# Hedgehog linear attention with a causal convolution gate on one core: value columns copied on GpSimd, batch 3's loads freed, the last output block in halves, and a new order of all work

## The chip, the cores and the metric

The kernel runs on one core of a Trainium2 chip. A core has five engines that run side by side, each through its own instruction queue in order: TensorE (PE, matmuls, with weight loads PEld shown apart), VectorE (DVE), ScalarE (ACT), GpSimd (POOL) and SyncE (SP, here a queue that issues DMAs). The metric is the device time of one execution in microseconds (us); the median of several runs counts.

## What is computed

There are 8 batches, 8 heads, 576 positions and head width 64; a feature map has 128 columns. Cut to what matters, the reference is:

```python
def phi(x):
    proj = einsum('bhsd,df->bhsf', x, w_phi)
    proj = proj - max(abs(proj), axis=-1, keepdims=True)
    return concatenate([exp(proj), exp(-proj)], axis=-1)
q_p, k_p = phi(q), phi(k)
kv  = einsum('bhsf,bhsd->bhfd', k_p, v);  z = sum(k_p, axis=2)
x   = einsum('bhsf,bhfd->bhsd', q_p, kv) / (einsum('bhsf,bhf->bhs', q_p, z)[..., None] + 1e-06)
x   = x.transpose(0, 2, 1, 3).reshape(B, S, 512)
gate = sigmoid(causal 5-tap convolution of x along s, one set of taps per column)
out  = (gate * (x @ w_val)) @ w_out
```

## The kernel before, in words

Each batch passes through the same chain of tasks. A batch's 4608 rows of q and of k lie as 18 chunks of 128 columns by 2 rows; `UNITS` groups the chunks into five units (four of 4 chunks and one of 2), so most tasks exist once per unit `u`. The names below are the ones the texts use, `name(b, u)` with batch and unit.

- q, k and v come by DMA (`load`, L550, on POOL for batches 1 to 7; `loadv`, L531, for v; `load32`, L525 and L527, on SP for batch 0). q and k must be transposed: in batch 0 and 1 by PE (`tp32`, `tp16`) with a copy out of PSUM (`tc32` L542 and L544, `tc16` L560), from batch 2 on by a transposing DMA (`xpose`, L565, on SP).
- `kp` and `qm` (L577, PE) project k and q with w_phi. `kmax` and `qmax` (L585, DVE) take the maxima of the absolute values. `kexp` (L595, ACT) takes exp of plus and minus the projection, so twice per unit. `ek` (L604, ACT) turns the maxima of k into factors, and `vs` (L610 and L611, POOL) scales v by them, four times per batch (head group, sign).
- `st` (L620, PE) sums k features times scaled v over positions; `kv` (L628 on DVE or L632 on ACT) brings the sums out of PSUM.
- The maxima of q are transposed by PE (`mqt`), negated by DVE (`mqr`, L667 in batch 0, L670 later) and spread by POOL (`rx`, L682; batch 0 may do one on DVE, L685). `qp` (PE) projects q again (L693) and adds the spread maxima (L698). `qexp` (ACT, L706; L709 for the last unit) takes the exps.
- `num` (L719, L726, PE) multiplies q features with the sums; `nrm` (L737, L740, DVE) divides. `xtp` (L748, L752, PE, or `xtd`, a DMA, L755) transposes x, `xtc` (L628 or L632) copies it out, `halo` (L768, L769, POOL) sets the convolution's edge columns.
- `gate` (L781, PE) is the convolution, 20 matmuls per column block `j`; `tanh` (L785, ACT) replaces the sigmoid; `val` (L791, PE) is x times w_val; `gv` (L797, DVE) multiplies the two; `gvc` (L805, POOL) gathers the last 32 rows of a batch.
- `out` (L813, PE) multiplies by w_out, four blocks of 128 positions per batch, and every second batch a fifth block (L817) for the remainders of two batches; `oev` (L630 on DVE or L634 on ACT) brings a block out of PSUM, halved; `odma` (L830, L836) stores it.

The weights for `val` are kept in `WV`, 512 columns and then the first 64 columns once more, because `val` reads 128 columns from a start that moves by 64. `c_wv` (L459, a DMA on POOL) loads the 512; `c_wvx` (L462) copies the extra 64. `c_wo` (L465) loads w_out, `c_dupo` (L469 to L471, three DMAs on SP) makes a shifted copy of it. `c_gt` (L486, POOL) builds the convolution's taps in two halves.

The order is not left to a scheduler at run time. `build` makes a list of some 1060 tasks with engines, planned durations and dependences; a planner that is not in the file has put them in a row, and the row is written out: `ORDER` lists the task numbers, `FLEX` gives a letter for every task that two engines could do (A for ACT, D for DVE, P for POOL), `BANKS` the PSUM banks, and `WARM` filler matmuls with no use but to keep PE busy, as "place:bank:size" ("z" fillers add zeros to a bank in use). The instructions are emitted in that row, so each engine's queue follows it. The dependences and durations in `build` only informed the planner: on the chip an instruction waits for the data and buffers that it truly uses, and for what stands ahead of it in its own queue. Where the text says "POOL does a, b, c", it is this row, filtered for POOL.

POOL before, around the loads of batch 3: `c_gt(1)`, `rx(1,4)`, `rx(1,3)`, `rx(1,0)`, `c_gt(0)`, `rx(1,1)`, `c_wv`, `rx(1,2)`, `holdx(2)` (a one-column copy, L512, that waits for batch 2's transposed q), `c_wo`, `vs(1,0,0)`, `vs(1,0,1)`, `load('q',3)`, `load('k',3)`, `vs(1,1,0)`, `halo(0)`, `vs(1,1,1)`, then the `rx` of batch 2. SP before: `xpose` of k and q of batch 2, `loadv(2)`, `c_wvx`, `c_dupo`, `xpose` of k and q of batch 3.

Of the kernel before, what the change touches and what calls it, by code (L numbers as in the profile page):

```python
# [18 lines left out]
DM = 512  # L19
P = 128  # L20
# [15 lines left out]
    "16:3:1 16:3:1 16:3:0 16:3:0 16:3:0 16:3:0 16:3:0 16:3:0 16:3:0 16:3:0 16:3:0 16:3:0 16:3:0 16:3:0 16:3:0 16:3:0 16:3:0 "  # L36
    "16:3:0 50:2:2 71:7:9 73:z80:1 76:0:1 82:z93:1 85:4:2 88:4:3 125:0:1 175:z232:1 181:6:1 191:4:2 206:0:1 216:2:1 "
# [42 lines left out]
)  # L80
FLEX = (
    "DADADAAAAADDPPPPDDDDAADDDDDDDDDDDDDAAADAAAADDDDAAADDDAADAAADDADAADDDDADDDDADDDDDDAADADDAAAAAA"
)
BANKS = (
    "672372616101454523232323016723676705012367230101455672345323010123454501452330176470701456745010145450145676723014501454"
    "501677014576601230167676745677773467232367232345456701676723232367674545014452353623670101232345454452230145450167676767"
    "010123014501230167450120167365012345236745454555723014545234567232323010123236745230167232346701432010167454567010120656"
    "701456701012301670123010167232367674567123677260123230123230167475644501016701670123676745672345232345450123670156672345"
    "010167452345742345670145670101674545012345012367452345010137452301670101452360167"
)  # L90


# [70 lines left out]
def build(plan, em=None):  # L163
# [16 lines left out]
    for b in range(B):  # L180
# [165 lines left out]
        for c in range(5):  # L346
            if c == 4 and b % 2 == 0:
                continue
# [550 lines left out]
```

## Time and profile before

| What | Value |
|---|---|
| Median of 3 runs | 214.34 us (213.82 to 215.61) |
| The profiled execution, its own time | 215.87 us |
| Its span, first to last instruction | 214.1 us |
| PE busy, share of the span | 193.5 us, 90% |
| ACT busy | 178.9 us, 84% |
| DVE busy | 170.3 us, 80% |
| POOL busy | 133.1 us, 62% |
| Bytes moved | 39.90 MB, mean 186 GB/s |
| Last matmul ends | about 208.5 us |

Rows of the profile are read like this. A timeline row gives the start, the duration, the engine and line, the operation, what it writes and reads, how many instructions were merged, and in brackets the idle time before them and what ended it; "issue" there means that the engine waited for nothing that the profile shows. A row of a group gives, behind the bar, busy time, mean ns of one, and the idle time before them. A row of DMA issues ends with the KB of one and the median us from issue to landing. A row of stages gives start and end, length, busy time and count for PE, PEld, DVE, ACT and POOL, then granted clock (1.00 is full), DMA share and GB/s.

### The profile page before, as it was taken

What the parts mean: (1) busy time and instruction counts of PE and PEld (TensorE: products, weight loads), DVE (VectorE), ACT (ScalarE), POOL (GpSimd) and SP (SyncE); (2) the same over time, 40 slices, a digit from 0 to 9 for tenths busy, and PEclk for the clock granted to TensorE, in tenths of its full rate; (3) what the DMA queues carried; (4) which work ended last, traced back from release to release, by engine and by line L of the source; (5) the groups of instructions that cost most, each with busy time, mean ns of one, the idle gap of its engine ahead of it and who ended that gap; (6) DMA issues with size and microseconds to landing.
All of it is one profiled execution on the core that took longest, in us unless ns stands there. A gap on an engine that the chain in (4) does not pass through costs nothing.

```text
span 214.1 us, 8769 instructions
## 1 busy us (share of the span) xinstructions
PE 193.5 (90%) x3809; PEld 137.1 (64%) x3829; DVE 170.3 (80%) x258; ACT 178.9 (84%) x265; POOL 133.1 (62%) x173
## 2 busy tenths in 40 slices
PE   7888687887999999989999999999999999999990
PEld 6554476565665866677667767567667756787630
DVE  3799979994899979988999779998699897653510
ACT  2899989996999899998899997998898988535250
POOL 3645999992957477954995199805991979110100
PEclk9999979999999999999999999999999999999999
DMA  6999989999699699999997979989961363872176
GB/s 194 355 265 210 305 147 202 240 200 193 131 181 271 103 154 269 281 190 162 214 287 133 150 137 275 160 181 207 254 207 45 88 196 73 124 163 65 52 208 184
DMA packets 49953, 39.90 MB, mean 186 GB/s; under 512 B 34165, under 2 KB 39541, under 8 KB 49914
## 3 DMA queue, kind: packets, MB, share of 16 engines
q1 hardware_dynamic: 43616, 28.65, 58.1%
q0 software_dynamic: 6032, 10.49, 26.0%
q8 instruction: 30, 0.49, 0.9%
q10 hardware_dynamic: 266, 0.21, 0.3%
q14 instruction: 9, 0.07, 0.1%
HBM read 30.48 MB, written 9.44 MB: 186 GB/s over the span
## 4 chain that ended last, share of the span: by engine, by line
PE 52%; ACT 19%; DVE 8%; DMA 8%; issue 6%; POOL 5%; SPq 0%; ACTq 0%; DVEq 0%; POOLq 0%
PE PS L791 12%; PE PS L813 10%; PE PS L781 9%; ACT QTIL L706 9%; ACT KTIL L595 7%; PE PS L719 6%; DMA VN<-in_v_dram 6%; PE PS L620 4%; POOL VT L610 3%; PE PS L577 3%; DVE MK L585 3%; PE PS L693 2%; PE PS L817 2%; DMA W<-in_w_phi_dram 2%; PE PS L698 2%
## 5 line engine op out<-in xcount | busy, mean ns | idle before, releaser
L595 ACT ACTIVATE KTIL<-PS 128x1024 bf16<-128x1024 f32 (+1 forms) x80 | 72.2, 968 | 3.9 <-PE PS L577 2.0
L610 POOL TENSOR_TENSOR VT<-VN,EK 128x1152 bf16<-128x1152 f32 x32 | 67.9, 2121 | 4.7 <-DMA VN<-in_v_dram 3.3
L706 ACT ACTIVATE QTIL<-PS 128x1024 bf16<-128x1024 f32 x64 | 62.9, 1056 | 1.4 <-PE PS L698 1.3
L682 POOL TENSOR_TENSOR RX<-MQR,ident 128x512 bf16<-128x512 bf16 (+1 forms) x39 | 36.6, 962 | 36.3 <-DVE MQR L670 34.2
L585 DVE TENSOR_REDUCE MK<-PS 128x8 f32<-128x1024 f32 (+1 forms) x40 | 43.9, 1111 | 2.4 <-ACT KTIL L595 1.4
L585 DVE TENSOR_REDUCE MQP<-PS 128x8 bf16<-128x1024 f32 (+1 forms) x40 | 43.4, 1109 | 1.2 <-PE PS L577 0.7
L791 PE MATMUL PS<-XT,WV 128*128 128x288 bf16 x256 | 34.8, 286 | 0.3 <-DVE KV L628 0.2
L797 DVE SCALAR_TENSOR_TENSOR GV<-TH,PS 128x576 bf16<-128x576 bf16 x32 | 23.8, 752 | 10.2 <-PE PS L791 4.6
L813 PE MATMUL PS<-WOUT,GV 128*128 128x512 bf16 x110 | 29.5, 380 | 1.1 <-issue 0.2
L791 PEld LDWEIGHTS <-WV 128*128 128x128 bf16 x256 | 23.8, 98 | 7.8 <-issue 1.3
L785 ACT ACTIVATE TH<-PS 128x576 bf16<-128x576 f32 x32 | 20.4, 664 | 9.1 <-PE PS L781 6.1
L620 PE MATMUL PS<-VT,KTIL 64*128 64x65 bf16 x1152 | 23.9, 194 | 1.6 <-POOL VT L611 0.6
L620 PEld LDWEIGHTS <-KTIL 64*128 64x128 bf16 x1152 | 21.7, 97 | 4.1 <-issue 2.6
L781 PE MATMUL PS<-XT,GW 64*64 64x288 bf16 x640 | 22.8, 285 | 0.8 <-DVE RCP L737 0.5
L740 DVE TENSOR_TENSOR XN<-PS,RCP 128x512 bf16<-128x512 f32 x32 | 22.1, 691 | 1.2
L719 PEld LDWEIGHTS <-QTIL 128*128 128x128 bf16 x512 | 18.2, 97 | 7.1 <-issue 4.9
L719 PE MATMUL PS<-KV,QTIL 128*128 128x65 bf16 x512 | 20.3, 194 | 0.8 <-ACT QTIL L706 0.5
L781 PEld LDWEIGHTS <-GW 64*64 64x64 bf16 x640 | 17.8, 106 | 3.0 <-issue 1.2
L634 ACT ACTIVATE OUTS<-PS 128x512 f32<-128x512 f32 x22 | 13.5, 620 | 7.3 <-PE PS L813 6.1
L813 PEld LDWEIGHTS <-GV 128*128 128x128 bf16 x128 | 11.2, 98 | 11.4 <-issue 0.6
L577 PE MATMUL PS<-W,qT 64*128 64x128 bf16 x288 | 15.3, 217 | 1.9 <-ACT KTIL L595 0.4
L577 PE MATMUL PS<-W,kT 64*128 64x128 bf16 x288 | 15.1, 223 | 1.9 <-DVE MQP L585 1.1
(79 smaller groups left out, 224.4 us busy)
## 6 DMA issues: line engine op xcount, KB each, us to landing
out_dram<-OUTS SPq DMA_DIRECT2D x32, 256.0 KB, 3.5
VN<-in_v_dram SPq DMA_DIRECT2D x7, 1152.0 KB, 6.6
KQN<-in_q_dram POOLq DMA_DIRECT2D x6, 576.0 KB, 8.4
KQN<-in_k_dram POOLq DMA_DIRECT2D x6, 576.0 KB, 10.0
KTIL<-in_k_dram SPq DMA_DIRECT2D x4, 288.0 KB, 4.1
VN<-in_v_dram POOLq DMA_DIRECT2D x1, 1152.0 KB, 19.3
KTIL<-in_q_dram SPq DMA_DIRECT2D x4, 256.0 KB, 5.1
out_dram<-OUTS SPq DMA_DIRECT2D x14, 64.0 KB, 2.8
```

The costliest lines, as they stand in the source:

```text
L577: nc.tensor.matmul(self.PS[:, t.grp.banks[par], i * P:(i + 1) * P], X[rows, (c0 + i) * P:(c0 + i + 1) * P], self.W2[rows, :], start=True, ...
L585: self.nc.vector.tensor_reduce(o, self.two(t.grp, n * P).rearrange("p a (c f) -> p a c f", f=F), AX.X, ALU.max, apply_absolute_value=True)
L595: self.nc.scalar.activation(self.KTIL[b % 2][:, s, c0:c0 + n, :, :].rearrange("p c a f -> p a c f"), self.two(t.grp, n * P).rearrange("p a ...
L610: nc.gpsimd.tensor_tensor(self.VT[g][:, s, :, 0:D], self.VN[b % 2][:, NC * g:NC * g + NC, :], e.to_broadcast([P, NC, D]), ALU.mult)
L620: nc.tensor.matmul(self.PS[:, t.grp.banks[ab], (s * 2 + x) * E1:(s * 2 + x + 1) * E1], self.KTIL[b % 2][rows, s, J // 2, J % 2, :], self.V ...
L682: self.nc.gpsimd.tensor_tensor(o, *wide(self.MQR[self.mq(b, u)][:, :], self.ident2), ALU.mult)
L706: self.nc.scalar.activation(o, i, AF.Exp, scale=1.0 - 2.0 * s)
L719: nc.tensor.matmul(self.PS[:, t.grp.banks[h // 4], (h % 4) * E1:(h % 4 + 1) * E1], Q[:, s, c % 2, h, (c // 2) * P:(c // 2 + 1) * P], self. ...
L781: self.nc.tensor.matmul(self.PS[o * D:(o + 1) * D, t.grp.banks[par], 0:R], self.GW[r, jj, 4 - m, :], X[r, 4 * a + jj, :, HALO - 8 * s:HALO ...
L791: self.nc.tensor.matmul(self.PS[:, t.grp.banks[par], 0:R], self.WV[:, i, (2 * j + par) * D:(2 * j + par + 2) * D], X[:, 4 * par + i, :, HA ...
L797: nc.vector.scalar_tensor_tensor(out=self.GV[b % 3][:, j, :, :], in0=self.TH[j][:, :, :], scalar=1.0, in1=self.two(t.grp, R), op0=ALU.add, ...
L813: nc.tensor.matmul(self.PS[:, t.grp.banks[0], :], GV[:, j, c % 2, (c // 2) * XH:(c // 2) * XH + P], self.WOUT[:, j, c % 2, :], start=(j == ...
```

## The change

Four things change in the code, and then the whole row of tasks.

1. `c_wvx` is a copy by GpSimd instead of a DMA on SP.
2. In the planner's dependences, batch 3's q and k loads no longer follow `c_wo`; both follow `holdx(2)`.
3. Batch 7's block 3 of the output is computed, brought out and stored in two halves of 256 columns (`outh`, `oevh`, `odmah`), each stored by SP or ACT as its letter says.
4. `FLEX` may now hold S for SP.
5. `ORDER`, `FLEX`, `BANKS` and `WARM` are new. The fillers go from 41 matmuls (18 places at the start, then 12) to 20 (17 at the start, then 3).

```diff
 WARM = (
-    "16:3:1 16:3:1 16:3:0 [16:3:0 fifteen times more] 50:2:2 71:7:9 73:z80:1 76:0:1 82:z93:1 85:4:2 88:4:3 125:0:1 175:z232:1 181:6:1 191:4:2 206:0:1 216:2:1 "
+    "16:6:1 16:6:1 16:6:0 [16:6:0 fourteen times more] 47:7:1 84:0:1 174:2:2 "
 )
...
-                    hx = A("lk", b, 1, "POOL", 0.85, fn("c_wo"), [hx], lat=0.6)
-                    cx = A("lk", b, 1, "DMA", 3.4, None, [hx])
+                    cx = A("lk", b, 1, "POOL", 0.85, fn("c_wo"), [hx], lat=0.6)
+                    cx = A("lk", b, 1, "DMA", 3.4, None, [cx])
...
-                    first = [hx] + first
...
-                cx = A("wvx", 0, 0, "SP", 0.56, fn("c_wvx"), [cx], rank=-440)
-                cx = A("wvx", 0, 0, "DMA", 2.0, None, [cx], rank=-440)
+                cx = A("wvx", 0, 0, "POOL", 0.4, fn("c_wvx"), [cx], rank=-440)
...
     def c_wvx(self, t):
-        self.nc.sync.dma_start(self.WV[:, :, DM:DM + D], self.WV[:, :, 0:D])
+        self.nc.gpsimd.tensor_copy(self.WV[:, :, DM:DM + D], self.WV[:, :, 0:D])
...
+    def outh(self, t, b, c, z):
+        GV = self.GV[b % 3]
+        for j in range(4):
+            self.nc.tensor.matmul(self.PS[:, t.grp.banks[0], 0:DM // 2], GV[:, j, c % 2, (c // 2) * XH:(c // 2) * XH + P],
+                                  self.WOUT[:, j, c % 2, z * DM // 2:(z + 1) * DM // 2], start=(j == 0), stop=(j == 3))
+    def oevh(self, t, b, c, z):
+        o = self.OUTS[out_seq(b, c) % NO][:, z * DM // 2:(z + 1) * DM // 2]
+        self.ev(t, o, self.PS[:, t.grp.banks[0], 0:DM // 2], 0.5)
+    def odmah(self, t, b, c, z):
+        eng = self.nc.scalar if t.eng == "ACT" else self.nc.sync
+        r = slice(z * DM // 2, (z + 1) * DM // 2)
+        d = self.out_d[b].rearrange("(k x y a) o -> a k y x o", k=2, x=8, a=2)[c % 2, c // 2, 0:16, :, r]
+        eng.dma_start(d, self.OUTS[out_seq(b, c) % NO][:, r])
```

The new row, put into words where the prediction speaks of it:

- DVE at the start: the copies of k's units 0 and 1, `kmax(0,0)`, `kmax(0,1)`, `qmax(0,0)`, `qmax(0,1)`, `kmax(0,2)`, `qmax(0,4)`, the first `mqr`, `qmax(0,3)`, `qmax(0,2)`, the copy of k's unit 4, the second `mqr`. Before: the copies of k's units 0 and 2, `kmax` 0 and 1, `qmax` 1 and 0, the copy of unit 4, the first `mqr`, `kmax` 3 and 2, `qmax` 3, 2 and 4, `kmax(0,4)`, the second `mqr`.
- POOL at the start: four `rx` of batch 0 and then its four `vs`; the fifth `rx` (unit 3) is on DVE. Before: two `rx`, one `vs`, two `rx`, three `vs`; the `rx` on DVE was that of unit 4.
- POOL around batch 3's loads: `rx(1,0)`, `rx(1,1)`, `c_gt(1)`, `c_wv`, `rx(1,4)`, `rx(1,2)`, `rx(1,3)`, `holdx(2)`, `vs(1,0,1)`, `load('q',3)`, `c_wo`, `vs(1,0,0)`, `load('k',3)`, `c_gt(0)`, `c_wvx`, `halo(0)`, `vs(1,1,1)`, `vs(1,1,0)`, then the `rx` of batch 2. SP: `xpose` of k and q of batch 2, `loadv(2)`, `c_dupo`, `xpose` of k and q of batch 3.
- From DVE to ACT, up to the last `qexp` of batch 7: output evictions on ACT 17 instead of 13, wide XT copies 3 instead of 2, narrow ones 3 instead of 2, `kv` 5 instead of 4, and the narrow copy of batch 1's q.
- End of PE: `out(7,2)`, the remainder block `out(7,4)`, then the two halves of block 3, second half first. Both halves are brought out by DVE; ACT stores the second half after its two stores of `out(7,4)`, SP the first half after its two.

More of the change, by code (lines that the diff above doesn't have):

```diff
@@ L35 @@
 WARM = (
-    "16:3:1 16:3:1 16:3:0 16:3:0 16:3:0 16:3:0 16:3:0 16:3:0 16:3:0 16:3:0 16:3:0 16:3:0 16:3:0 16:3:0 16:3:0 16:3:0 16:3:0 "
-    "16:3:0 50:2:2 71:7:9 73:z80:1 76:0:1 82:z93:1 85:4:2 88:4:3 125:0:1 175:z232:1 181:6:1 191:4:2 206:0:1 216:2:1 "
+    "16:6:1 16:6:1 16:6:0 16:6:0 16:6:0 16:6:0 16:6:0 16:6:0 16:6:0 16:6:0 16:6:0 16:6:0 16:6:0 16:6:0 16:6:0 16:6:0 16:6:0 "
+    "47:7:1 84:0:1 174:2:2 "
 )
@@ L43 @@
 ORDER = (
[36 rows of a table removed]
[36 rows of a table added]
 )
 FLEX = (
-    "DADADAAAAADDPPPPDDDDAADDDDDDDDDDDDDAAADAAAADDDDAAADDDAADAAADDADAADDDDADDDDADDDDDDAADADDAAAAAA"
+    "DDAADAAAAADDPPPDPDADADDADDDDDADADDDAAAAAADDADADAAADDDAAADAADDDDDAADAAAADADDDDDDDAAAAADDAAADDSDAA"
 )
 BANKS = (
[L85 to L89, printed above, removed]
+    "454616507701234523232323672345672305670167236767452670101123010123456701452370425445201456701010145670101016767456745454"
+    "501016456745267014501676745677773567232367452345676723012301232367674545015452343623670101232345454432230145450167672367"
+    "016767014501230167014530167264012345236745454555023014545234567232323010123236745230167230146701435010167234567010131666"
+    "701456701012301670123010167232367674567723676300123230123230167425544501016701670123676745234545232345450123450174670145"
+    "0101452345342523456701456767016745456723450123670123012367676701232301672345507502"
 )
@@ L147, in follow @@
     def follow(self):
-        names = {"A": "ACT", "D": "DVE", "P": "POOL"}
+        names = {"A": "ACT", "D": "DVE", "P": "POOL", "S": "SP"}
         for t, f in zip([t for t in self.tasks if len(t.engs) > 1], FLEX):
@@ L348, in build @@
                 continue
+            if b == B - 1 and c == 3:
+                for z in range(2):
+                    g = plan.group("out", 1)
+                    o = A("out", b, c, "PE", 0.44, fn("outh", b, c, z), [G("gv", b, j) for j in range(4)], g, 0)
+                    oe = A("oev", b, c, ("ACT", "DVE"), (act(256), dve(256)), fn("oevh", b, c, z), [o, oseq.get(out_seq(b, c) - NO)], g)
+                    od = A("odma", b, c, ("SP", "ACT"), (0.6, 0.6), fn("odmah", b, c, z), [oe])
+                    A("odma", b, c, "DMA", 0.5, None, [od])
+                h["out", b, c] = o
+                continue
             g = plan.group("out", 1)
```

72 rows, old and new, of the table ORDER are left out of this document.

## The prediction

> **What bounds the kernel now.** I read the page first, then a table of engine time by stage, then the chain of waits, then the rows around each place that the change touches.
>
> ```profile
> span 214.1 us, 8769 instructions
> ...
> PE 193.5 (90%) x3809; PEld 137.1 (64%) x3829; DVE 170.3 (80%) x258; ACT 178.9 (84%) x265; POOL 133.1 (62%) x173
> ...
> q8 instruction: 30, 0.49, 0.9%
> ```
>
> The profiled execution took 215.87 us: 214.1 of span and 1.77 around it. It is 1.53 above the median of 214.34. I sum differences, set them against 215.87, and move the result to the median.
>
> By stage (start:end length, then busy time of PE, weight loads, DVE, ACT, POOL, granted clock, DMA share, GB/s):
>
> ```profile
> 8.00:48.00 40.00, 31.99 (x635) 23.00 (x638) 38.20 (x55) 38.85 (x57) 34.60 (x38) 0.96 1.06 234
> 48.00:56.00 8.00, 6.44 (x174) 4.98 (x171) 5.31 (x7) 6.10 (x14) 3.99 (x6) 1.00 0.81 148
> 56.00:96.00 40.00, 38.21 (x824) 26.98 (x830) 35.30 (x54) 39.33 (x56) 28.56 (x35) 1.00 1.01 206
> 96.00:184.00 88.00, 86.76 (x1795) 60.69 (x1800) 77.37 (x118) 80.30 (x120) 60.96 (x74) 1.00 0.82 171
> ```
>
> Up to 96 us ACT sets the pace: it idles 1.15 us, 1.90 and 0.67 in the first three rows, 3.72 together. PE is short of work until about 56 us (8.0 idle in the first row, 1.6 in the second) and then full: 1.8 and 1.2 us idle in the last two. From 96 us PE alone sets the end, and ACT has 7.70 us to spare there. So a microsecond of PE saved before 56 us counts only if ACT, the loads and the maxima let PE go ahead.
>
> Two rows show where the early stretch is pinned. Batch 3's k arrives by a transposing DMA, and its first projection waits for it:
>
> ```profile
> 54.66 2.70 SPq L565 DMA_TRANSPOSE kT<-KQN  x1
> ...
> 61.24 0.11 PEld L577 LDWEIGHTS <-kT 64*128 64x128 bf16 x4 [0.24 <-DMA kT<-KQN]
> ```
> ```profile
> SPq L565 <- DMA KQN<-in_k_dram: 5.3, 1, 5.3
> ```
>
> The last line is SP's own wait in 49 to 56 us: the transpose is held 5.3 us by the load of that k. Projection kp(3,4) then waits only 0.24 us, so PE and this load come out even at 61.2 us. Whatever is won before that is lost again unless the load lands earlier too.
>
> **The change, part by part.**
>
> *Loads of batch 3 and the value columns, on POOL and SP.* POOL before:
>
> ```profile
> 33.04 1.25 POOL L486 TENSOR_TENSOR GW<-cwP,ID 128x640 bf16<-128x640 f32 x1
> ...
> 35.24 0.81 POOL L459 DMA_DIRECT2D WV<-in_moe_w_val_dram  x1
> ...
> 38.00 2.14 POOL L610 TENSOR_TENSOR VT<-VN,EK 128x1152 bf16<-128x1152 f32 x1
> ...
> 42.42 0.60 POOL L550 DMA_DIRECT2D KQN<-in_q_dram  x1
> 43.02 0.75 POOL L550 DMA_DIRECT2D KQN<-in_k_dram  x1
> ...
> 45.98 0.38 POOL L768 COPY XT<-XT 128x224 bf16<-128x224 bf16 x1
> ```
>
> One vs instruction pair takes 2.21 us here ((42.42 - 38.00) / 2). In the new order POOL does vs, load q, c_wo, vs, load k. If the first vs again starts at 38.00, q is issued at 40.21 (2.2 earlier), c_wo behind it at 40.81 instead of ahead of the first vs, and k at 38.00 + 2.21 + 0.60 + 0.81 + 2.21 = 43.83, which is 0.8 later than 43.02 (c_wo taken like c_wv, 0.81). So freeing the loads from c_wo frees q, not k. The vs needs ek(1), which has more ACT work ahead of it: a narrow copy, 0.38, and one more qexp, 62.9 / 64 = 0.98 (rows below). So k may be 0.8 to 2.2 late. Against that WOUT's load and its copies no longer run ahead of k. Before, k took 54.66 - 43.02 = 11.6 us.
>
> ```profile
> L706 ACT ACTIVATE QTIL<-PS 128x1024 bf16<-128x1024 f32 x64 | 62.9, 1056 | 1.4 <-PE PS L698 1.3
> ...
> KQN<-in_k_dram POOLq DMA_DIRECT2D x6, 576.0 KB, 10.0
> ...
> WOUT<-in_moe_w_out_dram POOLq DMA_DIRECT2D x1, 512.0 KB, 9.8
> ```
>
> With the median of 10.0 k lands at 53.8, with the old 11.6 at 55.4 to 56.8. On SP the transpose stands behind c_dupo: WOUT issued at 40.81 lands 9.8 later at 50.6, three issues follow at some 0.7 (the end's rows, below), so the queue is free near 53. I take 0 for the gate at 61.2, which lies between the two landings, with -0.9 and +2.1 as ends.
>
> The copy c_wvx leaves SP and becomes one POOL copy of 128x256 elements. The nearest row is the 0.38 of 128x224; I take 0.4, with 0.26 (the 18-wide VT cast, below) and 1.25 (c_gt, L486, 640 wide) as ends. WV is now issued ahead of three rx, so before 35.24; with WOUT's 9.8 it lands before 35.24 + 0.81 + 9.8 = 45.85. POOL reaches the copy after load k and c_gt(0), at 43.83 + 0.75 + 1.25 = 45.83, so it should not wait. Behind it stands halo(0), for which the four gates of batch 0 wait: 46.2 instead of 45.98. PE has other tasks queued before the gates, so 0, and up to 1.6 if the vs is late. SP lost nothing by its old copy: the next transpose waited for the load anyway.
>
> *Start.* DVE must now do kmax(0,2) and qmax(0,4) before the first mqr, and qmax(0,0) waits for q's chunk 0, evicted after four other ACT tasks.
>
> ```profile
> 12.15 0.41 DVE L542 CAST kT<-PS 128x256 bf16<-128x256 f32 x1
> ...
> 12.91 2.35 DVE L585 TENSOR_REDUCE MK<-PS 128x8 f32<-128x1024 f32 x2
> ...
> 18.03 0.68 DVE L585 TENSOR_REDUCE MK<-PS 128x4 f32<-128x512 f32 x1
> ```
> ```profile
> 18.40 2.12 POOL L610 TENSOR_TENSOR VT<-VN,EK 128x1152 bf16<-128x1152 f32 x1 [3.29 <-DMA VN<-in_v_dram]
> ...
> 29.11 0.26 POOL L611 CAST VT<-EK 128x18 bf16<-128x18 f32 x1
> ```
>
> The first mqr comes at least 1.18 + 0.68 - 0.41 = 1.4 us later (a wide and a narrow maximum more, one copy fewer), but the second has kmax(0,3) and kmax(0,4), 1.9 us, less ahead of it. POOL used to idle 3.29 us before v landed at 18.40; now four rx fill that time, and four vs at 2.21 follow, to about 28.5 to 29.5 by where the maxima let rx start, against 29.37. I take 0, ends -1 and +1.
>
> *Work moved from DVE to ACT.* Counting the engine letters up to the last qexp of batch 7, ACT gets four more output evictions, one wide and one narrow XT copy, one KV copy and the narrow q copy:
>
> ```profile
> L634 ACT ACTIVATE OUTS<-PS 128x512 f32<-128x512 f32 x22 | 13.5, 620 | 7.3 <-PE PS L813 6.1 <-PE PS L817 0.9 <-DMA out_dram<-OUTS 0.3
> ...
> L632 ACT CAST KV<-PS 128x520 bf16<-128x520 f32 x4 | 2.6, 658 | 0.0
> ...
> L632 ACT COPY XT<-PS 128x1024 bf16<-128x1024 bf16 x2 | 2.1, 1052 | 0.0
> ...
> L632 ACT COPY XT<-PS 128x256 bf16<-128x256 bf16 x3 | 1.1, 376 | 0.9 <-PE PS L752 0.9
> ```
>
> That is 4 x 0.62 + 1.05 + 0.66 + 2 x 0.38 = 4.95 us. Of it 1.05 + 0.38 = 1.43 lies before batch 3's last qexp, in the stretch where ACT has 3.72 us of idle time, half of which (the 1.90 at 48 to 56) hangs on PE's stall below. I take half of it, +0.7, ends 0 and +1.4. The other 3.5 lie under PE where ACT has 7.70 to spare: 0, ends -1.2 (PE's own idle time there, all that any order can win) and +1.7 (half of 3.5).
>
> *Fillers and the instruction fetch.* The fillers fall from 41 matmuls to 20, all in the gaps; as work they cost nothing, so 0. Removing them shifts PE's instruction stream. PE halts twice inside a group whose instructions wait for nothing new:
>
> ```profile
> 49.75 0.10 PEld L698 LDWEIGHTS <-ONES 64*128 64x128 bf16 x1
> 51.11 0.09 PEld L698 LDWEIGHTS <-ONES 64*128 64x128 bf16 x1 [1.27 <-issue]
> ```
> ```profile
> 94.92 0.72 PEld L620 LDWEIGHTS <-KTIL 64*128 64x128 bf16 x42 [0.64 <-issue]
> ```
> ```profile
> 0.00:50.20 50.20, 40.15 (x731) 29.16 (x734) 43.01 (x63) 44.19 (x63) 38.22 (x53) 0.97 1.02 234
> 50.20:94.45 44.25, 41.60 (x892) 29.49 (x895) 38.17 (x57) 42.04 (x65) 31.78 (x38) 1.00 0.97 196
> ```
>
> Between the halts lie 895 weight loads. The 30 instruction packets carry 3809 + 3829 instructions, 255 each, some 127 pairs of load and matmul; 895 is seven such packets. So I read the halts as late packets at load 734 and load 1629. In the new order these counts fall at the start of kp(2,2) and inside st(3,1), after almost the same tasks in the same crowded DMA stretch, so I expect them again: 0, ends -1.9 (both gone) and +0.6 (a third). The Trainium skill, Runtime: NRT & Kernel Launch, section Instruction fetch mechanics, has blocks of 256 instructions, as counted here, but calls the cost of a boundary mostly hidden. The 1.27 us speak against that; by the page alone neither halt would recur and the sum would be 212.9.
>
> *End.* Rows of the tail:
>
> ```profile
> 207.46 1.05 PE L817 MATMUL PS<-WOUT,GVT 128*64 128x512 bf16 x8
> ...
> 208.60 0.60 ACT L634 ACTIVATE OUTS<-PS 128x512 f32<-128x512 f32 x1 [0.44 <-PE PS L817]
> 209.23 1.42 SPq L836 DMA_DIRECT2D out_dram<-OUTS  x2
> ```
>
> Now the eight matmuls of L817 come before the two halves, about 0.9 us earlier, and PE still ends near 208.5. Their four stores start at 208.3 and fill SP's and ACT's queues, two each, until 209.8; the half stores stand behind them. The last issue begins at 209.8 instead of 209.23 + 0.71 = 209.94: -0.2 with the smaller eviction, ends -0.6 and +0.4.
>
> Sum: 0 + 0 + 0.7 + 0 + 0 - 0.2 = +0.5, so 216.4 for an execution like the profiled one and 214.8 for the median.
>
> **Rivals.**
>
> A, ACT becomes the pace-setter after 96 us too. Of the 4.95 us no more than the gaps that PE leaves can be hidden. If 60% of it shows, +3.0 - 0.2 gives 217.1. For it: 39.33 of 40 busy at 56 to 96 us. Against it: 7.70 idle after. It decides once ACT's idle time from 8 to 184 us (11.4 us) falls by less than 2.6.
>
> B, the clock drops again.
>
> ```profile
> 25.00:29.00 4.00, 2.59 (x54) 1.95 (x50) 3.64 (x7) 4.00 (x5) 4.00 (x3) 1.00 0.78 205
> 29.00:33.00 4.00, 3.59 (x123) 3.59 (x124) 3.19 (x5) 2.97 (x5) 4.00 (x6) 0.57 1.08 153
> ```
> ```profile
> 12.00:18.00 6.00, 5.01 (x59) 2.96 (x58) 5.80 (x8) 6.00 (x11) 2.04 (x2) 1.00 1.11 227
> ```
> ```profile
> 12.00:18.00 6.00, 1.95 (x7) 0.80 (x9) 1.00 1.11 227
> ```
>
> After four microseconds at 65% busy the granted clock was 0.57 for four, a loss of 4 x 0.43 = 1.7 us of PE. The last row is the fillers of L495 alone: without them 12 to 18 us falls from 84% to 51% busy, so one more such drop is likely enough. PE is not the bound there; if all of it shows, 214.8 + 1.7 = 216.5. The rule in the Trainium skill, TensorE: Matmul & The Clock Gate, section What's actually happening, is that idleness over a window of some 3.4 us halves the clock. The trace agrees with the half (0.57 with its edges), but shows it at 65% busy, not idle.
>
> C, the stalls go. Without the two halts (1.27 and 0.64), without the ACT term, and with k landing 0.9 earlier, 214.8 - 1.9 - 0.7 - 0.9 = 211.3. Against it: three things must go right at once, and the counts say the halts stay.
>
> D, the freed loads free nothing: k lands 2.1 us late and the gate at 61.2 moves by as much less PE's reordering, +1.2: 216.0.
>
> **How the numbers follow.** A measurement of this kernel can tell about 1% (2.1 us) from no change, so faster means below 212.2 and slower above 216.5. Forecast 0.42, D 0.10, both within 1%: 0.52. A 0.18 and B at its full price 0.10: slower 0.28. C, whole or mostly, 0.20. The range from 211.3 to 217.8 takes in C's and A's sums and leaves about 1 in 10 on each side.
>
> **What would show it.** Right: kp(3,4) starts within 1 us of 61.2 and again waits for kT; ACT idles less than 11.4 us from 8 to 184; PE halts near loads 734 and 1629; c_wvx takes about 0.4 with no wait for WV. Wrong: granted clock below 0.9 between 15 and 28 us (B); PE idle above 4 us from 56 to 184 with waits for ACT (A); no halts and k's transpose issued before 53 (C). The forecast fails most simply if the order after 96 us leaves PE waiting, which no row of before can show.

## The result, and the profile after

The changed kernel takes 222.35 us (median of 4 runs, 220.88 to 223.71), the kernel before 214.98 beside it. The ratio is 1.0337, 95% interval 1.0229 to 1.0445: slower by 3.4%, some 7.2 us, where 214.8 was predicted and the range ended at 217.8. Ratios here and below leave out executions over 1.5% above the fastest of their kernel, medians don't, so a median can lie above what its ratio says.

The profiled execution is the fastest of the four: 220.88, of it 219.1 span. It is 5.0 us longer than the profiled one of before, so 2 us of the loss do not show in this pair of traces: after's profiled run lies 1.5 us below its median, before's 0.9 above.

The page of after, first lines:

```profile
span 219.1 us, 8757 instructions
...
PE 192.8 (88%) x3796; PEld 136.4 (62%) x3812; DVE 169.1 (77%) x253; ACT 182.4 (83%) x271; POOL 133.2 (61%) x174
```

TensorE does the same work (192.8 against 193.5 us busy) in a longer span. By the stages of the prediction (length, busy time of PE, weight loads, DVE, ACT, POOL, granted clock, DMA share, GB/s):

```profile
8.00:48.00 40.00, 29.39 (x571) 20.61 (x572) 35.37 (x51) 38.59 (x58) 31.17 (x37) 0.91 1.04 230
48.00:56.00 8.00, 6.89 (x224) 5.67 (x218) 5.75 (x8) 7.63 (x14) 4.81 (x5) 1.00 1.11 188
56.00:96.00 40.00, 38.05 (x784) 26.70 (x788) 35.91 (x55) 38.62 (x56) 31.44 (x40) 1.00 1.05 207
96.00:184.00 88.00, 83.79 (x1713) 58.84 (x1716) 73.12 (x109) 80.51 (x120) 58.45 (x71) 1.00 0.81 165
```

The clock of the first row is 0.91 where before had 0.96. PE idles 1.95 and 4.21 us in the last two rows where before had 1.79 and 1.24, and only a small part of it for ScalarE. The longest waits of PE from 56 to 184 us (total, times, longest):

```profile
PE PS L627 <- issue: 1.8, 1, 1.8
PE PS L798 <- issue: 0.8, 1, 0.8
PE PS L788 <- ACT KTIL L602: 0.5, 1, 0.5
PE PS L726 <- ACT TH L792: 0.4, 1, 0.4
```

The two largest have no releaser; they are read here, as in the prediction, as halts of the instruction stream.

To place the loss, I compare when two runs have begun the same amount of TensorE work (each task weighted by its shortest time over the runs). By this measure after is 0.6 us behind before's profiled run at 60 us, 2.0 at 76, 2.9 at 96, 4.2 at 128 and 5.0 at 196. So the early part looked even, as predicted, and the loss seemed to lie behind 61 us. The experiments show that this reading was half wrong.

### The profile page after: what moved, and what is told of

Same layout as the page of the kernel before. It is cut to its first block, busy times and chain, and to the rows that moved or that the text cites. A ratio compares the mean times of both kernels' runs of the same rounds, so it can differ in the third digit from the quotient of the medians.

```text
span 219.1 us, 8757 instructions
## 1 busy us (share of the span) xinstructions
PE 192.8 (88%) x3796; PEld 136.4 (62%) x3812; DVE 169.1 (77%) x253; ACT 182.4 (83%) x271; POOL 133.2 (61%) x174
## 4 chain that ended last, share of the span: by engine, by line
PE 58%; DVE 19%; ACT 9%; issue 6%; DMA 5%; DVEq 0%; ACTq 0%
PE PS L798 14%; PE PS L820 9%; DVE MQP L592 8%; PE PS L627 6%; PE PS L788 6%; PE PS L726 6%; DVE MK L592 6%; PE PS L584 4%; DMA kT<-KQN 4%; ACT KTIL L602 4%; PE PS L700 4%; PE PS L705 3%; ACT QTIL L713 3%; PE PS L755 2%; DMA KTIL<-in_k_dram 1%
## 5 line engine op out<-in xcount | busy, mean ns | idle before, releaser
L713 ACT ACTIVATE QTIL<-PS 128x1024 bf16<-128x1024 f32 x64 | 62.1, 1041 | 0.9 <-PE PS L705 0.6
L592 DVE TENSOR_REDUCE MQP<-PS 128x8 bf16<-128x1024 f32 (+1 forms) x40 | 43.9, 1111 | 4.2 <-PE PS L584 3.4
L820 PE MATMUL PS<-WOUT,GV 128*128 128x512 bf16 x108 | 28.6, 379 | 1.2 <-issue 0.3
L641 ACT ACTIVATE OUTS<-PS 128x512 f32<-128x512 f32 x24 | 14.6, 621 | 7.2 <-PE PS L820 5.4
```

Of the source, the lines that this page charges most:

```text
L592: self.nc.vector.tensor_reduce(o, self.two(t.grp, n * P).rearrange("p a (c f) -> p a c f", f=F), AX.X, ALU.max, apply_absolute_value=True)
L713: self.nc.scalar.activation(o, i, AF.Exp, scale=1.0 - 2.0 * s)
L820: nc.tensor.matmul(self.PS[:, t.grp.banks[0], :], GV[:, j, c % 2, (c // 2) * XH:(c // 2) * XH + P], self.WOUT[:, j, c % 2, :], start=(j == ...
```

## The experiments

Theory 1: the new order loses time in three places behind 61 us (a GpSimd copy ahead of vs, a load of V ahead of two transposes, a longer halt). Theory 2: ScalarE has too much work, most of it moved behind 61 us. Theory 3: the missing fillers, by way of the clock. Theory 4: the code edits cost by themselves. Theory 5: the early order's own waits. In each diff below the lines are tasks of the order, not code, unless they read like code.

### Code edits alone, and three single repairs of after

**e1: before with the code edits alone.**

```diff
-SP:   c_wvx (DMA, ahead of c_dupo)
+POOL: c_wvx (tensor_copy, ahead of halo(0))
-out(7,3) oev(7,3) odma(7,3)           between out(7,1) and out(7,2)
+outh(7,3,1) outh(7,3,0) and their oevh, odmah     behind out(7,4)
```

> The order, queues, banks and fillers of before, with the code edits alone: the value columns copied on GpSimd just ahead of halo(0), and out(7,3) computed, evicted and stored last, in two halves. Theory 1 (the new order loses the time, in three places: halo(1) on GpSimd, loadv(6) on SyncE, a longer halt of instruction fetch): the edits cost nothing, 214 to 216 us. Theory 2 (ScalarE has too much work) and theory 3 (the missing fillers, by the clock) say the same, 214 to 216. Theory 4 (the edits cost the time themselves, the copy by holding GpSimd, the halves by a longer end): 218 us or more.

Measured 215.17 against 215.01, ratio 0.9984 (0.9936 to 1.0032). Theory 4 falls: the edits cost nothing that shows. The run also holds a surprise. It has before's early order, and its first stage and its kp(3,4), the gate of the prediction, are

```profile
8.00:48.00 40.00, 32.14 (x671) 22.73 (x677) 39.26 (x56) 39.64 (x59) 35.76 (x40) 1.00 1.12 235
```
```profile
59.15 0.11 PEld L588 LDWEIGHTS <-kT 64*128 64x128 bf16 x4 [0.48 <-DMA kT<-KQN]
```

a clock of 1.00, not 0.96, and kp(3,4) at 59.15, not 61.24. The profiled run of before had a clock drop and a halt of its own, 2.1 us of delay at the gate. e1's profiled run (213.77) lies 1.4 us below e1's median, as after's does below its own, and is the better partner: against it, after is 2.9 us behind at 60 us, not 0.6, and 7.1 at 196. The early part only looked even because before's profiled run had lost time there too.

**e2: load of V for batch 6 later.**

```diff
 qmax(5,1)
-loadv(6)
 kp(5,2)
...
 xpose(k,6)
...
 xpose(q,6)
+loadv(6)
```

> After, with the load of V for batch 6 moved behind batch 6's two transposes on SyncE, as before had it. Theory 1: the transpose of k lands within 7 us of its issue instead of 9.07, kp(6,4) waits less, and the time falls by 1.0 to 1.8 us, to about 221 where after is 222.3. Theories 2 and 3: the load is hidden and the time stays within 0.5 us of after. Rival inside theory 1: the transpose is late because its own source (load of k6) landed at 119.98, 2.5 us later than before, and lands no earlier; then 0 to 0.5.

Measured 221.53, ratio 1.0246 (1.0139 to 1.0352) where after had 1.0337: 0.9% less, 0.8 us by medians. By work done it loses 0.6 us from 116 to 128 us where after loses 1.7. That lies between what theory 1 asked for (1.0 to 1.8) and its rivals (at most 0.5), and the intervals overlap.

**e3: halo(1) behind vs.**

```diff
 load(q,4)
-halo(1)
 load(k,4)
 vs(2,0,0)
+halo(1)
 vs(2,0,1)
```

> After, with load k4 and vs(2,0,0) ahead of halo(1) in GpSimd's queue. Theory 1: GpSimd no longer stands 2.42 us for XT, the last vs(2) ends near 74 instead of 75.9 us, st(2,1,0) starts 1.4 to 2.0 us earlier than 78.1, and the time falls by 1.0 to 2.0 us. Theories 2 and 3: another wait takes its place and the time stays within 0.5 us of after.

Measured 223.52, ratio 1.035 (1.0252 to 1.0449), no gain. GpSimd did what was wanted (the profiled execution is the slowest of the four, 227.98, but by work done it is about 0.5 us behind after's at most up to 92 us):

```profile
64.53 0.75 POOL L558 DMA_DIRECT2D KQN<-in_k_dram  x1
65.28 2.14 POOL L618 TENSOR_TENSOR VT<-VN,EK 128x1152 bf16<-128x1152 f32 x1
...
73.25 0.25 POOL L619 CAST VT<-EK 128x18 bf16<-128x18 f32 x1
```

The last vs(2) ended at 73.5 us instead of 75.9, yet st(2,1,0) still started at 78.58 (78.11 in after). GpSimd's wait was real, and taking it away won nothing; st stands behind gate(1,2) in TensorE's queue (g3 below).

**e4: engine letters back.**

```diff
-FLEX: oev(1,3) oev(2,0) oev(3,1) oev(4,1) oev(4,3) kv(5,0) xtc(5,0) xtc(5,2) xtc(6,2) ... on ACT
+FLEX: the 20 letters behind 63 us that differ, as before has them (12 to DVE, 8 to ACT)
```

> After, with the 20 evictions behind 63 us that went to another engine sent back to the engine that before gave them (net 4 us of work from ScalarE to VectorE). Theory 2 (ScalarE overloaded): the time falls by 2 to 5 us. Theory 1: the letters move nothing that sets the pace, within 0.7 us of after. Theory 3: within 0.7 us.

Measured 224.06 (221.21 to 228.37), without an interval; its lowest run is above after's lowest, 220.88. Theory 2 asked for 217 to 220. It falls for the work behind 63 us: giving that back to VectorE wins nothing. The three tasks that ScalarE got ahead of 61 us stay with it in e4.

### New order and old order joined at a place

These take the first part of one order and the remaining tasks in the sequence of the other, with banks and letters of the order that each task comes from.

```diff
-order: new throughout
+h1: new up to kp(3,4) at 61 us, old behind it
+h2: old up to kp(3,4) at 61 us, new behind it
+h3: old up to kp(4,4) at 96 us, new behind it
+h4: old up to num(4,3) at 131 us, new behind it
```

> The new order (its queues, banks, engine letters and fillers) up to kp(3,4) at 61 us, and before's order from there. Measured by work done, after was 0.5 to 0.6 us late at that place. Theory 1 (the time is lost in stretches of the new order behind 61 us: 72 to 76, 94 to 96, 120 to 128): 215 to 216.5 us, no different from before. Theory 3 (the early part with few fillers sets what follows, by the clock or by where the halts of instruction fetch fall): 218 or more.

> Before's order and fillers up to kp(3,4) at 61 us, the new order from there. Theory 1: 218.5 to 221.5 us, nearly all of after's loss. Theory 3: about 215, since the fillers are back. Theory 2 (ScalarE has too much work, most of it moved behind 61 us): as theory 1.

> Before's order up to kp(4,4), which ended at 96 us, the new order from there. Left of after's loss by work done: 1.3 us at 120 to 128 and 0.7 later. Theory 1: 216.5 to 218 us; the stretch 72 to 76 and the longer halt at 96 are gone, the stretch at 120 to 128 stays. Theory 2: the same or more, since 4 of the 5 us moved to ScalarE lie behind 96 us: 217 to 219. Theory 3: 215.

> Before's order up to num(4,3) at about 131 us, the new order from there. Theory 1: 215 to 216.2 us, since after lost only 0.7 us more behind 130 us. Theory 2: 216 to 217.5, since most of the moved evictions lie here. Theory 3: 215.

Measured: h1 219.6, ratio 1.0225 (1.0202 to 1.0249); h2 217.87, 1.0123 (1.0090 to 1.0155); h3 218.91, 1.0178 (1.0126 to 1.0230); h4 218.36, 1.0087 (1.0037 to 1.0138). The two halves add up: 2.25% + 1.23% = 3.5%, after's 3.4%. But they add up the other way round from theory 1, which had asked for 215 to 216.5 in h1 and 218.5 to 221.5 in h2: nearly two thirds of the loss lies ahead of 61 us, where the two first profiles looked alike. h1's four runs show mean clocks of 0.974 to 0.978; the runs of before in the same comparisons mostly 0.984 to 0.998. That h3 is no cheaper than h2 says that the losses behind 61 us are not a plain sum either. And h4, which has only the part behind 131 us, loses 1.9 us by its ratio, where theory 1 had expected 0.7; no run takes that part asunder, so this stays open.

### The early part: fillers or order

```diff
 f1: old order with the code edits
-WARM: 12 of the 13 groups of fillers behind the 18 at the start
 f2: h1
+WARM: 30 units (of 256 columns) at mqt(0,1) 5, qm(1,0) 5, num(0,4) 3, xtp(0,2) 3, tp16(k,1) 3, ... each on that task's bank
```

> Before's order with the code edits (which cost nothing by themselves), and 12 of its 13 groups of early fillers left out, so that TensorE has as few in its gaps as in after. Theory 3 (the early loss of 4.7 us, which the new order showed up to 61 us, comes from the missing fillers by way of the granted clock): mean clock at or below 0.98, 217.5 to 219.6 us. Theory 5 (it comes from the order of the early work itself, whose waits leave TensorE idle, and the clock only follows or adds): clock near 0.99, 214.5 to 216.5.

> The new order up to 61 us and before's from there (219.6 us), with 32 units of fillers put into TensorE's longest early gaps, each on the bank of the task that follows. Theory 3: the clock holds, 215 to 216.5 us. Theory 5: the waits stay, the clock is back at 0.99, 217.5 to 219.6.

f1: 217.45, ratio 1.0085 (1.0040 to 1.0130), clocks 0.970 to 0.990. f2: 216.98, ratio 1.0114 (1.0044 to 1.0185), clocks 0.996 to 0.999. So taking the fillers out of the old order costs some 1.8 us by the ratio (0.9 to 2.8; 2.7 by medians), putting fillers into the new one wins 2.4 (2.25% less 1.14%), and 2.4 stay. Each time lies between what theories 3 and 5 asked for: both hold in part. Within f1, where nothing differs but the execution, the time goes with the clock: the four of its ten runs with a mean clock of 0.981 to 0.990 took 214.8 to 216.2 us, the six with 0.970 to 0.975 took 217.4 to 219.6. Stages 16 to 20 and 20 to 24 us, first of after, then of f1, h1, f2 (the clock stands third from the end; f1's profiled execution was 2.0 us behind e1's at 10 us already, ahead of the first filler that it lacks, so its rows show the clock and not its price):

```profile
16.00:20.00 4.00, 2.35 (x30) 1.12 (x26) 4.00 (x7) 4.00 (x7) 2.44 (x4) 1.00 1.18 217
20.00:24.00 4.00, 3.58 (x44) 2.33 (x38) 3.30 (x4) 3.99 (x11) 4.00 (x3) 0.71 1.14 218
```
```profile
16.00:20.00 4.00, 2.82 (x30) 1.63 (x30) 3.99 (x5) 3.85 (x8) 2.93 (x3) 0.72 1.18 213
20.00:24.00 4.00, 3.79 (x36) 2.84 (x35) 3.32 (x7) 3.46 (x10) 3.48 (x5) 0.50 1.09 203
```
```profile
16.00:20.00 4.00, 2.61 (x30) 1.14 (x25) 4.00 (x7) 4.00 (x5) 3.23 (x4) 1.00 1.16 213
20.00:24.00 4.00, 3.31 (x34) 2.13 (x34) 3.84 (x6) 3.64 (x12) 3.21 (x3) 0.60 1.14 221
```
```profile
16.00:20.00 4.00, 3.22 (x28) 1.66 (x28) 3.48 (x7) 4.00 (x8) 2.68 (x4) 1.00 1.16 213
20.00:24.00 4.00, 3.31 (x47) 2.04 (x46) 4.00 (x6) 3.58 (x11) 3.82 (x3) 1.00 1.14 222
```

In after and h1 TensorE is busy 2.35 and 2.61 of 4 us, and the clock falls to 0.71 and 0.60; in f1 it is down from 16 us on. In f2, with 3.22 busy, it holds. This is rival B, in the new order and, without fillers, in the old one too.

The 2.4 us that stay come with the new early order and its fillers. Ahead of kp(3,4) TensorE has the same tasks in both orders. From 8 us up to kp(3,4), first in e1, then in f2:

```profile
8.00:59.15 51.15, 42.19 (x889) 29.84 (x892) 47.36 (x70) 50.26 (x75) 43.86 (x48) 1.00 1.10 220
```
```profile
8.00:61.83 53.83, 42.53 (x893) 30.13 (x892) 46.33 (x66) 51.94 (x79) 41.30 (x46) 1.00 1.03 215
```

VectorE (third) is not what fills up: it has 1.0 us less to do in f2 and idles more. ScalarE (fourth) is nearly full in both, idle for 0.89 us in e1 and 1.89 in f2, and it has 1.7 us more to do, since the new letters give it the wide XT copy xtc(0,1), kv(1,1) and the narrow copy of q there (1.08, 0.59 and 0.37 us in f2). So of the 2.7 us by which f2 reaches kp(3,4) later, 1.7 are ScalarE's added work. This is no accident of two executions: ScalarE is busy 50.2 to 50.8 us up to kp(3,4) in the nine kept traces with before's early order and fillers, which reach it at 59.2 to 61.2 us, and 51.9 to 52.9 us in the seven with all of the new early order, which reach it at 61.1 to 63.0.

Two things are not settled by this. No run sends these three letters back, so what they cost in time is read from traces and not tested. And the fillers have a price of their own: those of f2 hold TensorE for 6.20 us from 8 to 61 us where those of e1 hold it for 3.71, and nine units too many cost 1.2 us in g4 below, so part of the 2.4 us may be theirs. Nor do the traces show the fillers' gain at kp(3,4): the new order reaches it at 61.1 to 63.0 us without them (after, e2, e3, e4, h1) and at 61.8 and 62.6 with them (f2, f4). That gain rests on the times of h1 and f2. Which half of the early order costs, g1 and g2 were to say:

```diff
+g1: new order, filled, up to kp(2,1) at 34 us, old behind it
+g2: old up to kp(2,1), new and filled up to kp(3,4) at 61 us, old behind it
```

> The new order with added early fillers up to kp(2,1) at 34 us, before's order from there. The new order up to 61 us still cost 2.2 us when filled. If that comes from its first half (waits for MK, MQP and qT between 8 and 34 us): 216.5 to 217.5 us. If from the second half (waits for XN, XNT, TH and MK between 34 and 61): 214.5 to 215.8.

> Before's order up to kp(2,1) at 34 us, the new order with added fillers from there to kp(3,4) at 61 us, before's order from there. The opposite of the last: 214.5 to 215.8 us if the first half costs, 216.5 to 217.5 if the second half does; 215.5 to 216.5 in both if the cost is spread.

g1: 218.3, ratio 1.0175 (1.0114 to 1.0235). g2: 217.25, 1.0129 (1.0073 to 1.0185). g1 is above both of its ranges, g2 lies where a costly second half had been expected (216.5 to 217.5); of the three tasks moved to ScalarE, g2 has the two larger ones. Together (3.0%) they cost more than both halves in one kernel (1.1%), so the joint at 34 us may cost something itself, or part of one hides the other. This stays open.

```diff
 g4: old order with the code edits
+WARM: 9 units more, at kp(0,4) 2, qm(1,3) 2, kp(1,3) 2, num(0,3) 1, xtp(0,2) 1, st(1,0,0) 1
```

> Before's order with the code edits and 9 more units of fillers in TensorE's early gaps. If the granted clock still costs before something in most of its runs (its mean is 0.984 to 0.998 over runs): 213.5 to 214.5 us and a clock of 0.995. If fillers beyond before's are of no use or hold up the work behind them: 215 to 216.

g4: 215.78, ratio 1.0054 (1.0016 to 1.0091). No version came out of this that beats before: more fillers than before's cost half a per cent.

### Behind 61 us

```diff
+g3: old up to kp(3,4), new up to kp(4,0) at 84 us, old behind it
```

> Before's order, with the new order from kp(3,4) at 61 us to kp(4,0) at 84 us alone. After lost 1.2 us by work done at 72 to 76 us, where gate(1,2) waits for the banks of kp(3,3). If it is lost for good: 215.8 to 216.5 us. If the rest makes up for it (one run with the new order from 61 us had lost it again by 96): 214.3 to 215.3.

g3: 216.48, ratio 1.0077 (1.0039 to 1.0115), lost for good. The place, in rows of g3's TensorE, ScalarE and VectorE:

```profile
73.58 0.81 PE L790 MATMUL PS<-XT,GW 64*64 64x288 bf16 x20 [0.49 <-ACT KTIL L604]
```
```profile
72.50 1.02 ACT L604 ACTIVATE KTIL<-PS 128x1024 bf16<-128x1024 f32 x1 [0.63 <-DVE MK L594]
```
```profile
68.98 2.36 DVE L594 TENSOR_REDUCE MQP<-PS 128x8 bf16<-128x1024 f32 x2
71.26 1.22 DVE L594 TENSOR_REDUCE MK<-PS 128x8 f32<-128x1024 f32 x1
72.62 2.36 DVE L594 TENSOR_REDUCE MQP<-PS 128x8 bf16<-128x1024 f32 x2
```

Read from the first row down: gate(1,2) (L790) waits for banks 4 and 5, which hold kp(3,3). The exp of ScalarE that empties them stands behind their maximum (MK) in the row and is released by it, and VectorE has two q maxima (MQP), 1.2 us each, ahead of that. The new order projects qm(3,3), kp(3,3) and qm(3,0) in a row there; before had two gates, which ScalarE empties, ahead of kp(3,3).

```diff
 f3: h3
-loadv(6)     ahead of xpose(k,6)
+loadv(6)     behind xpose(q,6)
 g5: h2, with the same move
 g6: e1
-loadv(6)     behind xpose(q,6)
+loadv(6)     ahead of kp(5,2)
 f4: after with f2's fillers and the move of f3
```

> Before's order up to 96 us, the new one from there (218.9 us), with the load of V for batch 6 behind batch 6's two transposes. Theory 1 (the early load holds up the load and the transpose of k6, and kp(6,4) waits): the transpose of k6 lands before 123 us, kp(6,4) no longer waits, 215.5 to 217 us. Rival (the load of V is hidden, and the new order itself is late there): 218 to 219.

> Before's order up to 61 us, the new one from there (217.9 us), with the load of V for batch 6 behind the two transposes. If that load is most of what the new order loses behind 61 us beside the 1.2 us at 72 to 76: 215.8 to 217 us. If other waits take its place: 217.5 to 218.5.

> Before's order with the code edits, and one task moved: the load of V for batch 6 ahead of batch 6's transposes on SyncE, where the new order has it. If that place alone costs what it cost in the new order, by a later load or transpose of k6: 216.5 to 218.5 us, with TensorE standing at kp(6,4). If before's order has more slack there: 214.5 to 215.8.

> After with both repairs: the 32 units of early fillers, and the load of V for batch 6 behind the transposes. Theories 1 and 3 together: 4 us from the fillers and 1 to 2.5 from the load, 216 to 218.5 us where after is 222.3. Theories 1 and 5: 219.5 to 221.5.

f3: 216.9, ratio 1.0047 (1.0002 to 1.0093) where h3 had 1.0178. g5: 218.67, 1.0165 (1.0100 to 1.0231) where h2 had 1.0123. g6: 215.55, 1.0005 (0.9959 to 1.0050). f4: 218.86, 1.0183 (1.0112 to 1.0254) where after had 1.0337.

In the traces the mechanism is plain. SP's queue and kp(6,4), first in h2, then in g5:

```profile
113.84 0.37 SPq L540 DMA_DIRECT2D VN<-in_v_dram  x1
...
117.71 5.13 SPq L574 DMA_TRANSPOSE kT<-KQN  x1
```
```profile
126.70 0.11 PEld L586 LDWEIGHTS <-kT 64*128 64x128 bf16 x4 [2.16 <-DMA kT<-KQN]
```
```profile
118.77 3.42 SPq L574 DMA_TRANSPOSE kT<-KQN  x1
```
```profile
126.16 0.11 PEld L586 LDWEIGHTS <-kT 64*128 64x128 bf16 x4 [0.24 <-issue]
```

With the 1152 KB of V under way, k's transpose is 5.13 us in issue and lands after 8.95; without, 3.42 and 5.40, and the wait of 2.16 us goes. The times do not follow as plainly: by ratios the move wins 2.8 us in f3 and 2.0 in e2, loses 0.9 in g5, and its opposite costs nothing in g6. In g6 the load of V had landed 2.8 us after the transpose was issued (118.34 and 115.50), in h2 4.3 after (122.05 and 117.71), and kp(6,4) did not wait in g6. So the wait is shown, and that the later load takes it away; what that is worth in after's time stays open. g5, at 218.67, is above both of its ranges (215.8 to 217, or 217.5 to 218.5).

The two repairs in f4 win 3.3 of after's 7.2 us (1.54%), and 3.9 stay, about what the waits of the early order (2.4 in f2) and the stretch at 72 us (1.7 in g3) make together. That the sums agree proves neither: in f4's trace, of the slowest of its four executions, the halt at 98 us in after is gone too (below), so what f4 wins need not all be the two repairs'.

## Why the prediction was wrong

Point by point, by its own steps.

**Loads of batch 3 and the copy of the value columns: right.** GpSimd in after:

```profile
41.28 0.60 POOL L557 DMA_DIRECT2D KQN<-in_q_dram  x1
41.88 0.75 POOL L472 DMA_DIRECT2D WOUT<-in_moe_w_out_dram  x1
...
44.84 0.80 POOL L557 DMA_DIRECT2D KQN<-in_k_dram  x1
...
46.87 0.40 POOL L469 COPY WV<-WV 128x256 bf16<-128x256 bf16 x1
```

Each issue lies 1.0 to 1.1 us behind the worked-out time, and the copy takes 0.40 with no wait. That k landed at 54.00 (53.8 worked out) is in part luck: it was issued 1.0 us later and took 9.2 us instead of the 10.0 taken.

**The gate at 61.2: the size right, the meaning wrong.** kp(3,4) started at 61.78, within the microsecond asked for, though without waiting for kT, which had been asked for as well:

```profile
61.78 0.12 PEld L584 LDWEIGHTS <-kT 64*128 64x128 bf16 x4
```

But it was taken for a pin, where PE and the load come out even whatever happens ahead. Before's order passed it at 59.15 in e1, the new one at 63.01 in h1. The load is queued behind the same early work, so early time is not evened out there; it goes through to the end: by work done h1 is 4.5 us behind e1 at 60 us and 4.5 at 196. This is the misreading under the whole sum: a place that depends on what is ahead of it was taken for one that absorbs it.

**Fillers, "as work they cost nothing, so 0": wrong, 1.8 to 2.4 us by the times of f1 and f2.** The work was priced, its effect on the clock was left to rival B, with a chance of 0.10 and "PE is not the bound there". B came true: 0.71 at 20 to 24 us where it asked for below 0.9. Its price of 1.7 lies near f1's 1.8, whose interval is wide (0.9 to 2.8), and was not made up for later, since the gate absorbs nothing. The evidence lay in the prediction itself: fillers made 12 to 18 us 84% busy instead of 51%.

**Start, 0 within 1 us: right, as far as it reaches.** In after the first mqr starts at 14.39, 1.6 us later than in before (1.4 or more worked out), and the last vs of batch 0 ends at 28.87 (28.5 to 29.5). With the clock held, f2 is 0.9 us behind e1 at 28 us by work done, and 3.3 at 60. That loss lies between the start and kp(3,4), where the sum had no term but that for ScalarE, below.

**Halts: the places right, the sizes too small.** In after:

```profile
53.39 0.28 PEld L584 LDWEIGHTS <-kT 64*128 64x128 bf16 x10 [0.88 <-issue]
```
```profile
98.20 0.28 PEld L627 LDWEIGHTS <-KTIL 64*128 64x128 bf16 x14 [1.92 <-issue]
```
```profile
128.67 0.11 PEld L798 LDWEIGHTS <-WV 128*128 128x128 bf16 x2 [1.11 <-issue]
```

The first two stand at the start of kp(2,2) and inside st(3,1), at loads 734 and 1630, as counted. Together they take 2.80 against 1.91 us, +0.9 where +0.6 was the upper end, and there is a third of 1.11 at load 2270. In after these are the only three of over 0.5 us behind 48 us, and each lies a multiple of 128 loads behind load 94. The halt at 1630 is 1.81 and 1.93 us in e2 and e3 too, 0.6 to 1.1 (at 1629 or 1630) in most of the other traces and not to be seen in four of them, f4 with its 20 fillers more ahead among these. So the places are set by the count, but which of them show, and how long, is not; the second microsecond at 1630 is a part of after's loss that no run here isolates. The Trainium skill, Runtime: NRT & Kernel Launch, section Instruction fetch mechanics, calls the cost of a block boundary mostly hidden. Of some 25 boundaries behind 48 us three show in after, for 0.9 to 1.9 us each.

**Work moved to ScalarE, +0.7: too small, about 1.7 us by the traces.** The prediction took half of 1.43 us, because ScalarE had 3.72 us of idle time up to 96. Most of that was the accident of one execution: up to kp(3,4) ScalarE idles 3.05 us in before's profiled run and 0.89 in e1's, so there was hardly a gap to hide work in. And the 1.43 is a net figure up to batch 3's last qexp: ahead of kp(3,4) it is the three tasks of f2's rows, 2.0 us, of which some goes back to VectorE only behind it. The sign of failure was a bad one too: ScalarE's idle time from 8 to 184 us fell by 0.8, which by the prediction meant rival A, ScalarE as pace-setter after 96 us. e4 speaks against A: ScalarE idled there because TensorE was late. An idle sum tells of overload only if nothing else delays the engine.

**The order behind 56 us, 0 with ends -1.2 and +1.7: wrong, 2.6 us (h2).** The bounds came from the idle time of PE in before and from the evictions moved. Neither bounds what a new order can add. Banks held for VectorE (g3) and a load beside a transpose (h2, g5) had no term. The last sentence of the prediction named this as the simplest way to fail, and gave it no price.

**End: right.** From the last matmul's end to the end of the span 5.5 us, 5.6 before:

```profile
212.59 1.05 PE L849 MATMUL PS<-WOUT,GV 128*128 128x256 bf16 x8
...
215.29 0.56 SPq L860 DMA_DIRECT2D out_dram<-OUTS  x1
```

So the code edits came out as worked out, and the order around them, which was priced only where an edit touched it, cost all of the 7 us: by ratios 2.3% ahead of 61 us and 1.2% behind. Of the early part about half goes with the missing fillers by the times of h1 and f2, and the other half goes, as the traces read, mostly with ScalarE's added work, which no run tested.

## What to carry to other kernels

A profile of one execution has its own accidents: compare a stage with a second execution of the same kernel before calling it even, or a place in it a pin. A filler matmul is priced by the clock it keeps, and not only by its work: look at TensorE's busy share with and without it over the 4 us before each drop. Idle time of a nearly full engine in one execution is not slack: see whether a second execution has it too. When a whole instruction order is replaced, price each engine's queue against what the other engines wait for, or widen the range; joining old and new order at a quiet place locates the loss in a few runs.

## What the hardware showed that I had not expected

The clock drop is not fixed by the busy share over 4 us alone. The same order with the same share, 2.62 of 4 us at 24 to 28 us, first in before, then in e1:

```profile
24.00:28.00 4.00, 2.62 (x43) 1.89 (x41) 4.00 (x9) 4.00 (x5) 4.00 (x5) 1.00 0.69 266
28.00:32.00 4.00, 3.40 (x103) 3.20 (x102) 2.83 (x5) 2.97 (x5) 4.00 (x5) 0.65 1.01 181
```
```profile
24.00:28.00 4.00, 2.62 (x46) 1.97 (x44) 3.96 (x8) 4.00 (x5) 3.89 (x5) 1.00 1.48 326
28.00:32.00 4.00, 3.60 (x169) 3.12 (x167) 3.68 (x5) 4.00 (x7) 4.00 (x5) 1.00 0.81 155
```

In one the clock fell to 0.65, in the other it stayed, as it did behind 2.52 of 4 us in f2. So a schedule near this share can run with the drop in one execution and without in another. The 81 executions of before beside the experiments have mean clocks of 0.979 to 0.999, and 73 of them lie between 213.1 and 216.5 us; how much of that spread is the clock's was not measured. The Trainium skill, TensorE: Matmul & The Clock Gate, section What's actually happening, speaks of an idle window of some 3.4 us. The stretches here were two thirds busy, and in no trace here does TensorE idle for more than 2.8 us at a time between its first matmul and its last.

A transpose by DMA took 8.95 us beside a 1152 KB load and 5.40 without (h2, g5), and its issue held SyncE 5.13 us instead of 3.42.
